# An attention kernel whose V comes in 4 KB rows for three packs in four

## The chip, the cores and the metric

One core of a Trainium2 chip. The time is the device time of one execution in microseconds, lower is better. Where several were timed, the median is given.

## The reference

Two independent attention blocks, A and B, with the same shapes; their outputs are put side by side. For each block:

```python
B, Sq, D, H, Sk, Dh = 16, 64, 640, 32, 512, 128          # all bf16
q = (x @ wq).reshape(B, Sq, H, Dh).transpose(0, 2, 1, 3)
scores = einsum("bhqd,bhkd->bhqk", q, k_cache) * Dh**-0.5
p = softmax(scores, axis=-1)
o = einsum("bhqk,bhkd->bhqd", p, v_cache)
return o.transpose(0, 2, 1, 3).reshape(B, Sq, H * Dh) @ wo
```

The K and V caches are 268 MB together and each byte is used once; this is a kernel that reads.

## The kernel before

Work is cut into 128 packs: two batch rows and four heads each. 32 packs make a phase (16 heads of one block); four phases. Within a phase the pack index `j = n % 4` says which four heads. Each engine has a fixed program; a planner written in Python orders every operation by a guessed time (`AT`, in units of one pack) and derives the waits. The order of the loads on the SP queue is fixed too: the planner simulates the loader with guessed load times and takes, of the loads whose buffer it thinks free, the most urgent.

```python
    AT = dict(..., KT=(-1.051, -0.379), S=0, ..., PV=1.655, ...)
    DMA_US = dict(LDK=1.27, LDV=1.35, LDWQ=1.75, LDWO=1.75, LDX=0.45)
...
            ready = n - cfg.NK + AT["S"] + 0.25 if n >= cfg.NK else -99.0     # NK = 6 packs of K
            loads.append((tk - 0.05, ready, 2, op))
...
            ready = n - cfg.NV + AT["PV"] + 0.2 if n >= cfg.NV else -99.0     # NV = 4 packs of V
            loads.append((tv - 0.05, ready, 3, op))
```

V is laid out so that one row of a transfer is 2 KB, and P times V uses two 64-row tiles of the array:

```python
        def em_LDV(e, op):
            ...
            src = blocks[blk][2][2 * bp + b, h:h + 4].rearrange("(a s) (p t) d -> (s p) a (t d)", s=2, t=8)
            ins = e.dma_start(v_ring[:, n % NV, b].rearrange("p a t d -> p a (t d)"), src)
...
            ...
        def em_PV(e, op):
            ...
            for a in range(2):
                for b in range(2):
                    for t in range(8):
                        for s in range(2):
                            rows = slice(64 * s, 64 * s + 64)
                            col = a * 128 + 64 * b
                            last = e.matmul(o_ps[:, s, col:col + 64], v_ring[rows, n % NV, b, a, t, :],
                                            pT_ring[rows, (2 * n + a) % NT, b, t, :],
                                            start=(t == 0), stop=(t == 7), tile_position=(64 * s, 0))
                            ...
```

K comes as `"h (p t) d -> (h p) (t d)", t=16`: 4 KB rows. PE's program is a prologue, a loop of four packs run 31 times, and an epilogue:

```python
            for op in prog[:lo]:
                emit(e, op, p, {})
            with e.Fori(0, reps):
                ...
            ...
```

Of the kernel before, what the change touches and what calls it, by code (L numbers as in the profile page):

```python
# [17 lines left out]
class Cfg:  # L18
# [5 lines left out]
    NWS = 4  # L24
    NQ = 2
    NP = 2
    NPN = 2
    NT = 2
    NO = 1
    NR = 4  # L30
    PERIOD = 4
    FIRST = 5
    SLOT_US = 5.6
    AT = dict(XT=-2.594, XE=-2.103, XC=-0.826, QP=-0.625, QE=-0.284, KT=(-1.051, -0.379), S=0,
              EX=(0.262, 0.298, 0.389, 0.649), RC=(0.547, 0.697), NM=(0.571, 0.642, 0.8, 1.158), TR=(1.059, 1.236),
              TE=(1.121, 1.538), PV=1.655, OE=1.933, OP=2.167, OA=2.291, OV=2.255, ST=3.374, WP0=-1.75, WP1=-1.488)
    DMA_US = dict(LDK=1.27, LDV=1.35, LDWQ=1.75, LDWO=1.75, LDX=0.45)
# [22 lines left out]
def build_plan(dims, cfg, general):  # L60
# [17 lines left out]
    if not general:  # L78
        add("pool", "INIT1", 0, -10.0, [], [("out_sb", 0)])
        add("pool", "INIT2", 0, -9.9, [("out_sb", 0)], [("ident",)])  # L80
    for g in range(N // NJ + 1):
        n0 = g * NJ
        txt = n0 + AT["XT"]
        add("pe", "XT", g, txt, [("xn", g % cfg.NXN), ("ident",)], [("OUTB",)])
        if g == N // NJ:
            break
        if dims["FIRST"](g // NBP):
            add("act", "XE", g, n0 + AT["XE"], [], [("OUTB",), ("xs", g % NBP)])
            op = add("sp", "LDX", g, txt - 0.5, [], [("xn", g % cfg.NXN)])
            loads.append((txt - 2.4, (g - cfg.NXN) * NJ + AT["XT"] if g > cfg.NXN else -7.0, 0, op))  # L90
        add("pool", "XC", g, n0 + AT["XC"], [("xs", g % NBP)], [("xT", g % cfg.NX)])
    for ph in range(NPH):
        for j in range(NJ):
            w = ph * NJ + j
            n0 = ph * PH + j
            twp = n0 + (AT["WP1"] if ph else AT["WP0"])
            add("pool", "WP", w, twp, [("ws", w % cfg.NWS)], [("wqp", j)])
            op = add("sp", "LDWQ", w, twp - 0.5, [], [("ws", w % cfg.NWS)])
            ready = -99.0
            if w >= cfg.NWS:  # L100
                pw = w - cfg.NWS
                ready = (pw // NJ) * PH + pw % NJ + (AT["WP1"] if pw // NJ else AT["WP0"]) + 0.5
            loads.append((twp - 0.3 if not ph else ready + 2.0 + 0.15 * PH, ready, 1, op))
            tuse = n0 + AT["OE"]
            op = add("sp", "LDWO", w, n0 + AT["OP"] - 0.8 * NJ, [], [("wo", j)])
            ready = n0 - NJ + AT["OP"] + 0.2 if ph else -99.0
            loads.append((tuse - 0.3, ready, 4, op))
    for n in range(N):
# [3 lines left out]
        add("pe", "QP", n, n + AT["QP"], [("xT", g % cfg.NX), ("wqp", j)], [("SB", 0)])  # L112
        add("act", "QE", n, n + AT["QE"], [], [("SB", 0), ("qs", n % cfg.NQ)])
        for b in range(2):
# [3 lines left out]
            ready = n - cfg.NK + AT["S"] + 0.25 if n >= cfg.NK else -99.0  # L118
# [7 lines left out]
        for i in range(4):  # L126
            h = 4 * n + i
            te = n + AT["EX"][i]
            if general:
                add("dve", "MX", h, te - 0.002, [], [("SB", i), ("negmax", h % cfg.NR)])  # L130
            add("act", "EX", h, te, [("negmax", h % cfg.NR)] if general else [],
                [("SB", i), ("p", (h // 2) % cfg.NP, h % 2), ("rs", h)])
            add("pool", "NM", h, n + AT["NM"][i], [("p", (h // 2) % cfg.NP, h % 2), ("recip", (h // 2) % cfg.NR)],
                [("pn", (h // 2) % cfg.NPN, h % 2)])
        for a in range(2):
            m = 2 * n + a
            add("dve", "RC", m, n + AT["RC"][a], [("rs", 2 * m), ("rs", 2 * m + 1)], [("recip", m % cfg.NR)])
            add("pe", "TR", m, n + AT["TR"][a], [("pn", m % cfg.NPN, 0), ("pn", m % cfg.NPN, 1), ("ident",)],
                [("B5",)])
            add("dve", "TE", m, n + AT["TE"][a], [], [("B5",), ("pT", m % cfg.NT)])  # L140
        add("pe", "PV", n, n + AT["PV"], [("pT", (2 * n) % cfg.NT), ("pT", (2 * n + 1) % cfg.NT),
                                          ("v", n % cfg.NV, 0), ("v", n % cfg.NV, 1)], [("B5",), ("OUT1",)])
        add("act", "OE", n, n + AT["OE"], [], [("B5",), ("OUT1",), ("oT", n % cfg.NO)])
        add("pe", "OP", n, n + AT["OP"], [("oT", n % cfg.NO), ("wo", j)], [("OUTB",), ("OUT1",)])
        last = j == NJ - 1
        bp = g % NBP
        add("dve", "OA", n, n + AT["OA"], [("acc", bp, 1)],
            [("OUT1",), ("out_sb", 0) if last and final else ("acc", bp, 1)])
        if last:
            add("dve", "OV", g, n + AT["OV"], [("acc", bp, 0)],  # L150
                [("OUTB",), ("out_sb", 1) if final else ("acc", bp, 0)])
            if final:
                add("act", "ST", g, n + AT["ST"], [("out_sb", 0), ("out_sb", 1)], [("out_dram", g)])
    if not general:
        add("dve", "FL1", 0, N - 1 + AT["RC"][1] + 0.002, [("rs", h) for h in range(4 * N)], [("good",)])
        add("pe", "FLM", 0, N - 1 + AT["TR"][1] + 0.002, [("good",)], [("SB", 0)])
# [37 lines left out]
    lo = next(i for i, o in enumerate(pe) if o.kind == "TR" and o.idx == cfg.FIRST)  # L194
    hi = next(i for i, o in enumerate(pe) if o.kind == "TR" and o.idx == cfg.FIRST + 2 * cfg.PERIOD)
# [3 lines left out]
    step = dict(XT=cfg.PERIOD // NJ, QP=cfg.PERIOD, S=cfg.PERIOD, TR=2 * cfg.PERIOD, PV=cfg.PERIOD, OP=cfg.PERIOD)  # L199
# [7 lines left out]
    for op in ops:  # L207
        if op.kind == "OP":
            at[("OE", op.idx)].deps += [d for d in op.deps if d.kind == "LDWO"]
            op.deps = [d for d in op.deps if d.kind != "LDWO"]  # L210
        if op.kind == "XT" and op.idx > 0:
            hosts = [d for d in op.deps if d.kind == "OV"]
            for d in op.deps:
                if d.kind == "LDX" and hosts:
                    hosts[0].deps.append(d)
            if hosts:
                op.deps = [d for d in op.deps if d.kind != "LDX"]
# [3 lines left out]

    own = {"XC", "QE", "KT", "NM", "TE", "OE", "OA", "OV", "LDV"}

    def for_pe(d):
        if d.kind == "EX":
            return d.idx % 2 == 0
        if d.kind == "OV" and d.idx == N // NJ - 1 or d.kind == "OA" and d.idx == N - 1:
# [3 lines left out]
    def stand_in(d, op):  # L231
        if op.eng == "pe":
            if d.kind == "XE":
                return at[("OE", d.idx * NJ - NJ)] if d.idx else d
# [7 lines left out]
        if d.kind == "NM":  # L242
            return at[("TR", d.idx // 2)]
        if d.kind == "KT":
            return at[("S", d.idx[0])]
        if d.kind == "EX":
            return at[("EX", d.idx + 1)]
        if d.kind in ("OA", "OV"):
            n = d.idx if d.kind == "OA" else d.idx * NJ + NJ - 1
            return at[("OP", n + 1)]  # L250
        if d.kind == "OE":
            return at[("OP", d.idx)]
        if d.kind == "TE":
            return at[("PV", d.idx // 2)]
# [170 lines left out]
def mha_kernel(nc, blocks, out, cfg=None):  # L425
# [4 lines left out]
    assert SQ == 64 and DH == 128 and SK == 512 and D % 128 == 0 and B % 2 == 0 and H % 4 == 0  # L430
    KT = D // 128
    scale = float(DH) ** -0.5
    N0 = min(D, 512)
    N1 = D - N0
    assert 0 < N1 <= 128
# [5 lines left out]
    NH = NBLK * NBP * H  # L441

    plans = []
    for general in (False, True):
        dims = dict(NPH=NPH, NBP=NBP, NJ=NJ, FIRST=lambda ph: ph % NSUB == 0,
                    FINAL=lambda ph: ph % NSUB == NSUB - 1)
        plans.append(build_plan(dims, cfg, general))
    NK, NV, NKT, NX, NXN, NWS, NQ, NP, NPN, NT, NO, NR = (cfg.NK, cfg.NV, cfg.NKT, cfg.NX, cfg.NXN, cfg.NWS, cfg.NQ,
                                                          cfg.NP, cfg.NPN, cfg.NT, cfg.NO, cfg.NR)

    with contextlib.ExitStack() as es:
# [7 lines left out]
        ws_ring = sb("ws_ring", [128, NWS, KT, 512], BF16)  # L459
        kn_ring = sb("kn_ring", [128, NK, 2, 2048], BF16)  # L460
        kt_ring = sb("kt_ring", [128, NKT, 2, 16, 2, 32, 2], BF16)
        v_ring = sb("v_ring", [128, NV, 2, 2, 8, DH], BF16)
# [4 lines left out]
        p_ring = sb("p_ring", [128, NP, 8, 2, 64], BF16)  # L467
        pn_ring = sb("pn_ring", [128, NPN, 8, 2, 64], BF16)
        pT_ring = sb("pT_ring", [128, NT, 2, 8, 64], BF16)
        oT_ring = sb("oT_ring", [128, NO, 2, 2, 128], BF16)  # L470
# [3 lines left out]
        negmax = sb("negmax", [128, NR], F32)  # L474
        recip = sb("recip", [128, NR, 2], F32)
# [12 lines left out]
        PT_BANK, O_BANK, OUT_BANK = 4, 5, 7  # L488
        pt_flat = ps[:, PT_BANK:PT_BANK + 2, :].bitcast(BF16)[:, :, 0:512]
        o_ps = ps[:, O_BANK:O_BANK + 2, :].rearrange("p e c -> p (e c)")[:, 256:768].rearrange("p (s c) -> p s c", s=2)  # L490
        x_ps = ps[:, OUT_BANK, :].bitcast(BF16)
        out_ps0 = ps[:, OUT_BANK, 0:N0]
        out_ps1 = ps[:, O_BANK + 1, 256:256 + N1]
# [14 lines left out]

        def em_LDX(e, op):
# [5 lines left out]
        def em_LDWQ(e, op):  # L515
            c = op.idx % (NSUB * NJ)
            src = blocks[op.idx // (NSUB * NJ)][3].rearrange("(kt p) n -> p kt n", p=128)[:, :, c * 512:(c + 1) * 512]
            ins = e.dma_start(ws_ring[:, op.idx % NWS], src)  # L518
# [15 lines left out]
        def em_LDV(e, op):  # L534
            n, b = op.idx
            blk, bp, j, h = pack_info(n)
            src = blocks[blk][2][2 * bp + b, h:h + 4].rearrange("(a s) (p t) d -> (s p) a (t d)", s=2, t=8)
# [318 lines left out]
```

## Time and profile before

| | before |
|---|---|
| time | 770.06 us (3 runs, 769.87 to 770.34) |
| span of the profiled run | 768.0 us |
| DMA from 100 to 700 us | 395 GB/s, every 19.2 us slice but the last 90% busy or more, or nearly (the first is 8) |
| PE busy | 88% |
| last load lands, and the rest to the end | 756.7 us, 11.3 us |

PE is the engine of the matmuls and PEld its weight loads; DVE, ACT and POOL are VectorE, ScalarE and GpSimd. A ring is a set of buffers used in turn. The tail is the time from the landing of the last load to the end.

In the profile, a line of digits has one digit for each fortieth of the span, in tenths of busy time. "SPq" is the queue that issues loads; its time in the chain of waits means that transfers ahead of it had to be moved first. Landings and packets are single records of the trace. The prediction shows the lines themselves.

### The profile page before, as it was taken

How to read it: one execution, taken by the hardware profiler on the slowest of the kernel's cores; microseconds unless marked ns; L12 is line 12 of the kernel's file. 1: busy time of each engine (PE TensorE's matmuls, PEld its weight loads, DVE VectorE, ACT ScalarE, POOL GpSimd, SP SyncE). 2: the span in 40 equal slices, each digit the busy share in tenths (PEclk: the TensorE clock that was granted, in tenths of full speed). 3: DMA queues.
4: the chain of work that ended last, by engine and by line, in shares of the span. 5: the costliest groups of instructions: out<-in, count | busy, mean ns of one | idle time of the engine just before them, and what ended most of it. 6: DMA issues, size and time to landing. Idle time of an engine off the chain costs nothing.

```text
span 768.0 us, 44433 instructions
## 1 busy us (share of the span) xinstructions
PE 675.2 (88%) x20006; PEld 491.6 (64%) x20134; DVE 545.6 (71%) x934; ACT 483.8 (63%) x1297; POOL 405.9 (53%) x582
## 2 busy tenths in 40 slices
PE   3868999999987799999996779999998799999995
PEld 2546666676765567676765557676766567677764
DVE  3537777777765678787775567777877578788874
ACT  2536676776665567666764557677766566666763
POOL 5525545454954355554694344555568354545452
PEclk9989999999999999999999999999999999999999
DMA  8999999999999999999999999999999999999991
GB/s 312 388 385 386 398 397 398 396 397 398 397 385 388 388 398 400 399 399 399 397 393 391 383 391 397 396 387 398 398 398 391 391 399 398 400 399 399 400 396 60
DMA packets 130094, 295.16 MB, mean 384 GB/s; under 512 B 9216, under 2 KB 31744, under 8 KB 130048
## 3 DMA queue, kind: packets, MB, share of 16 engines
q1 hardware_dynamic: 127744, 292.06, 100.6%
q10 hardware_dynamic: 2304, 2.62, 1.0%
q8 instruction: 12, 0.20, 0.1%
q14 instruction: 34, 0.28, 0.1%
HBM read 292.03 MB, written 2.62 MB: 384 GB/s over the span
## 4 chain that ended last, share of the span: by engine, by line
SPq 55%; DMA 21%; PE 18%; issue 3%; DVE 1%; POOL 0%; ACT 0%; DVEq 0%
SPq L538 26%; SPq L531 25%; DMA v_ring<-in_A_v_cache_dram 11%; DMA v_ring<-in_B_v_cache_dram 6%; PE ps L659 5%; PE ps L573 4%; PE ps L596 3%; PE ps L675 2%; PE ps L640 2%; SPq L512 2%; DMA wo_sb<-in_B_wo_dram 2%; DMA kn_ring<-in_B_k_cache_dram 2%; DMA wo_sb<-in_A_wo_dram 1%; PE ps L678 1%; SPq L518 1%
## 5 line engine op out<-in xcount | busy, mean ns | idle before, releaser
L631 POOL TENSOR_SCALAR pn_ring<-p_ring,recip 128x512 bf16<-128x512 bf16 x512 | 345.7, 695 | 343.3 <-DVE recip L626 343.3
L611 ACT ACTIVATE p_ring<-ps 128x512 bf16<-128x512 f32 x512 | 301.0, 593 | 165.5 <-PE ps L640 162.5
L586 DVE STREAM_TRANSPOSE kt_ring<-kn_ring 128x1024 f32<-128x1024 f32 x256 | 314.5, 1232 | 102.6 <-DMA kn_ring<-in_B_k_cache_dram 56.3
L647 DVE COPY pT_ring<-ps 128x1024 bf16<-128x1024 bf16 x256 | 176.0, 687 | 54.4 <-PE ps L640 47.6
L573 PE MATMUL ps<-xT_ring,wqp_sb 128*128 128x128 bf16 x2560 | 171.0, 223 | 7.9 <-POOL xT_ring L562 5.5
L659 PE MATMUL ps<-pT_ring,v_ring 64*128 64x64 bf16 x8192 | 143.1, 191 | 23.9 <-DMA v_ring<-in_A_v_cache_dram 10.4
L573 PEld LDWEIGHTS ps<-xT_ring,wqp_sb 128*128 128x128 bf16 x2560 | 150.5, 115 | 15.6 <-POOL xT_ring L562 5.7
L659 PEld LDWEIGHTS ps<-pT_ring,v_ring 64*128 64x128 bf16 x8192 | 127.8, 95 | 41.6 <-DMA v_ring<-in_A_v_cache_dram 16.0
L596 PE MATMUL ps<-kt_ring,qs_ring 32*64 32x512 bf16 x4096 | 147.6, 399 | 4.6 <-issue 2.4
L640 PEld LDWEIGHTS ps<-ident,pn_ring 64*128 64x128 bf16 x4096 | 74.6, 95 | 118.7 <-ACT oT_ring L666 60.2
L666 ACT ACTIVATE oT_ring<-ps 128x512 bf16<-128x512 f32 x128 | 76.5, 598 | 99.0 <-PE ps L659 80.6
L678 PE MATMUL ps<-wo_sb,oT_ring 128*128 128x128 bf16 x512 | 112.5, 220 | 21.3 <-issue 18.8
L640 PE MATMUL ps<-ident,pn_ring 64*128 64x64 bf16 x4096 | 105.1, 192 | 26.9 <-DVE pT_ring L647 20.0
L675 PE MATMUL ps<-wo_sb,oT_ring 128*128 128x512 bf16 x384 | 118.8, 381 | 0.0
L611 ACT ACTIVATION_READ_ACCUMULATOR p_ring<-ps 128x1 f32 x512 | 101.7, 199 | 0.0
L675 PEld LDWEIGHTS ps<-wo_sb,oT_ring 128*128 128x128 bf16 x512 | 50.0, 98 | 53.1 <-issue 0.8
L579 ACT ACTIVATE qs_ring<-ps 128x512 bf16<-128x512 f32 x128 | 76.4, 597 | 10.8 <-PE ps L573 10.8
L596 PEld LDWEIGHTS ps<-kt_ring,qs_ring 32*64 32x64 bf16 x4096 | 55.5, 104 | 38.8 <-issue 4.0
L688 DVE TENSOR_TENSOR acc<-acc,ps 128x128 f32<-128x128 f32 x96 | 27.4, 285 | 32.9 <-PE ps L678 32.8
L678 PEld LDWEIGHTS ps<-wo_sb,oT_ring 128*128 128x128 bf16 x512 | 50.4, 98 | 0.0
L626 DVE RECIPROCAL recip<-rowsum 128x2 f32<-128x2 f32 x256 | 35.6, 139 | 2.6 <-ACT p_ring L611 2.6
L545 POOL COPY wqp_sb<-ws_ring 128x1280 bf16<-128x1280 bf16 x16 | 20.0, 1252 | 8.1 <-DMA ws_ring<-in_A_wq_dram 8.1
(24 smaller groups left out, 116.4 us busy)
## 6 DMA issues: line engine op xcount, KB each, us to landing
kn_ring<-in_A_k_cache_dram SPq DMA_DIRECT2D x128, 512.0 KB, 12.5
v_ring<-in_A_v_cache_dram SPq DMA_DIRECT2D x128, 512.0 KB, 12.6
kn_ring<-in_B_k_cache_dram SPq DMA_DIRECT2D x128, 512.0 KB, 12.6
v_ring<-in_B_v_cache_dram SPq DMA_DIRECT2D x128, 512.0 KB, 10.7
ws_ring<-in_A_wq_dram SPq DMA_DIRECT2D x8, 640.0 KB, 11.7
wo_sb<-in_A_wo_dram SPq DMA_DIRECT2D x8, 640.0 KB, 12.2
ws_ring<-in_B_wq_dram SPq DMA_DIRECT2D x8, 640.0 KB, 12.2
wo_sb<-in_B_wo_dram SPq DMA_DIRECT2D x8, 640.0 KB, 12.6
```

The costliest lines, as they stand in the source:

```text
L531: ins = e.dma_start(kn_ring[:, n % NK, b, :], src)
L538: ins = e.dma_start(v_ring[:, n % NV, b].rearrange("p a t d -> p a (t d)"), src)
L573: last = e.matmul(ps[:, 0, f * 128:(f + 1) * 128], w[:, kt, f, :], xT_ring[:, xs, kt, :], start=(kt == 0), stop=(kt == KT - 1))
L586: ins = e.transpose(dst, kn_ring[:, n % NK, b, :].bitcast(F32))
L596: last = e.matmul(ps[64 * b:64 * b + 64, i, :], qs_ring[rows, n % NQ, f, b, :], kt_ring[rows, n % NKT, b, :, f // 2, :, f % 2], start=(f = ...
L611: ins = e.activation(dst, src, ACTF.Exp, scale=1.0, accum_out=rowsum[:, h:h + 1])
L631: ins = e.tensor_scalar(pn_ring[:, (h // 2) % NPN, :, h % 2, :], p_ring[:, (h // 2) % NP, :, h % 2, :], recip[:, (h // 2) % NR, h % 2:h % ...
L640: last = e.transpose(pt_flat[:, b, 64 * t:64 * t + 64], pn_ring[rows, op.idx % NPN, t].rearrange("q s k -> q (s k)"), ident[rows, rows], t ...
L647: ins = e.tensor_copy(pT_ring[:, op.idx % NT].rearrange("p b t q -> p b (t q)"), pt_flat)
L659: last = e.matmul(o_ps[:, s, col:col + 64], v_ring[rows, n % NV, b, a, t, :], pT_ring[rows, (2 * n + a) % NT, b, t, :], start=(t == 0), st ...
L675: last = e.matmul(out_ps0, oT, wo_sb[:, 4 * j + h4, 0:N0], start=(j == 0 and h4 == 0), stop=(j == NJ - 1 and h4 == 3))
L678: last = e.matmul(out_ps1, oT, wo_sb[:, 4 * j + h4, N0:D], start=(h4 == 0), stop=(h4 == 3))
```

## The change

The intent: V's rows of 2 KB cost more DMA time per byte than K's of 4 KB, and DMA binds. For `j` in 0, 1, 2 V is now laid out as K is. The 4 KB rows put a head on 32 partitions, so P times V is done by four 32-row tiles. The change puts the results of the four row tiles in four PSUM banks. Two of these are shared with the output projection, which keeps accumulating in them; in these two the part for P times V is zeroed by ScalarE and accumulated into without a start flag. wq comes in 4 KB rows in three of the four phases.

```diff
+    PAD = 80
+    WIDE = (0, 1, 2)
-    AT = dict(..., KT=(-1.051, -0.379), S=0, ..., PV=1.655, OE=1.933, OP=2.167, ...)
-    DMA_US = dict(LDK=1.27, LDV=1.35, LDWQ=1.75, LDWO=1.75, LDX=0.45)
+    AT = dict(..., KT=(-1.24, -1.0), S=0, ..., PV=1.75, OE=(2.0, 2.06), ZO=2.11, OP=2.31, ...)
+    DMA_US = dict(LDK=1.27, LDV=1.29, LDWQ=1.5, LDWO=1.75, LDX=0.45)
...
-            ready = n - cfg.NK + AT["S"] + 0.25 if n >= cfg.NK else -99.0
+            ready = n - cfg.NK + AT["KT"][b] + 0.25 if n >= cfg.NK else -99.0
...
         def em_LDV(e, op):
...
+            if j in WIDE:
+                ins = e.dma_start(dst.rearrange("p t d -> p (t d)"), src.rearrange("h (p t) d -> (h p) (t d)", t=16))
+            else:
+                ins = e.dma_start(dst.rearrange("p (a t) d -> p a (t d)", a=2), ...)          # as before
...
         def em_PV(e, op):
...
+            tall, tiles, per = (32, 4, 16) if wide else (64, 2, 8)
+            for a in range(4 // tiles):
+                for b in range(2):
+                    for t in range(per):
+                        for s in range(tiles):
+                            rows = slice(tall * s, tall * s + tall)
+                            i, c = a * tiles + s, a * per + t
+                            last = e.matmul(ps[:, 4 + i, 64 * b:64 * b + 64], v_ring[rows, n % NV, b, c, :],
+                                            pT_sb[rows, b, c, :], start=(t == 0 and i < 2), stop=(t == per - 1),
+                                            tile_position=(tall * s, 0), skip_group_check=i >= 2)
...
+        def em_ZO(e, op):
+            ins = e.activation(z_ps, zeros[:, :].rearrange("p (s c) -> p s c", s=2), ACTF.Copy)
...
         def em_LDWQ(e, op):
...
+            if ph:
+                ins = e.dma_start(ws_sb[:, i].rearrange("p j c -> p (j c)"), src[:, i, c:c + NJ * 512])
...
         def run_program(e, eng, p):                        # PE only
+            for _ in range(0 if p else cfg.PAD):
+                e.sem_inc(s_fl, 1)
```

Beside these, all transposes of a pack are one run of 32, the exps of wide packs write plain rows, and the output is added up once in four packs.

## The prediction

> **What bounds the kernel now.** I first read the busy line of the DMA engines over the span, then the packets.
>
> ```profile
> PE   3868999999987799999996779999998799999995
> ...
> DMA  8999999999999999999999999999999999999991
> GB/s 312 388 385 386 398 397 398 396 397 398 397 385 388 388 398 400 399 399 399 397 393 391 383 391 397 396 387 398 398 398 391 391 399 398 400 399 399 400 396 60
> DMA packets 130094, 295.16 MB, mean 384 GB/s; under 512 B 9216, under 2 KB 31744, under 8 KB 130048
> ```
>
> The DMA line is 9 from the second slice (19.2 us each) to the last but one; PE dips to 6 and 7 near slices 12, 22 and 31, where a new set of weights is loaded. The chain of waits agrees:
>
> ```profile
> SPq 55%; DMA 21%; PE 18%; issue 3%; DVE 1%; POOL 0%; ACT 0%; DVEq 0%
> ```
>
> 76% of it is the load queue and its transfers. The list of waits says that the queue itself hardly waits for buffers (PV 1.9 us, scores 0.8 us, 20.5 us for the small x buffer, with transfers still queued behind it). So the rings always have room, and the time is the sum of what the 16 DMA engines move, plus a start and an end. Bytes don't change; only cost per byte can.
>
> That cost I took from the packet records of the trace. Mean durations: 1024 B 50.6 ns, 1280 B 58.9, 2048 B 87.9, 4096 B 164.7. Packets of one engine overlap by about 4 ns (an engine starts 2048 B packets every 80 ns though each shows 84). A least-squares fit of packet counts in 1 to 4 us windows against elapsed time gives 46.9, 55.4, 84.3 and 161 ns. With these the DMA work is 747.5 us of the 768.0, leaving 20.5 for start and end. The landing times are a second measure: K (512 KB in 4 KB rows) lands a median 1.282 us after the load before it (mean 1.299), a pair of V (2 KB rows) 2.706 (mean 2.752), so 1.353 each; wq (640 KB in 1 KB rows) 1.857.
>
> PE is second, and close. From the timeline of one undisturbed pack:
>
> ```profile
> 154.26 1.11 PE L659 MATMUL ps<-pT_ring,v_ring 64*128 64x64 bf16 x64
> ...
> 155.30 1.14 PE L596 MATMUL ps<-kt_ring,qs_ring 32*64 32x512 bf16 x32
> ...
> 156.37 0.41 PE L640 MATMUL ps<-ident,pn_ring 64*128 64x64 bf16 x16
> ...
> 157.90 0.41 PE L640 MATMUL ps<-ident,pn_ring 64*128 64x64 bf16 x16
> ...
> 158.24 1.31 PE L573 MATMUL ps<-xT_ring,wqp_sb 128*128 128x128 bf16 x20
> ...
> 159.54 1.11 PE L659 MATMUL ps<-pT_ring,v_ring 64*128 64x64 bf16 x64
> ```
>
> PV to PV is 5.28 us with PE nearly solid. Starts of PV run 5.25, 5.4, 5.27, 5.5 (mean 5.36) away from weight loads and 7.1 beside them. K and V of one pack cost DMA 2 x 1.282 + 2.706 = 5.27. Inside a phase of 32 packs PE and DMA are therefore about level; weights, x and output put DMA ahead as the bound.
>
> **What the Trainium skill says.**
> 1. "Perfetto Trace Analysis", DMA Optimizations: going from 2 KB to 4 KB or more "can dramatically improve throughput". The trace agrees in direction; its own gain is only 2 x 84.3 against 161, under 5%.
> 2. "DMA: Bandwidth & Descriptors", Why small descriptors are slow: some 3 cycles of overhead per packet on top of one per 32 B. By that estimate 2 x 67 cycles become 131, 2.2%; the trace shows about twice that, and I use the trace.
> 3. "TensorE: Matmul & The Clock Gate", Part 3, The mechanism: matmuls on different row tiles start about 4 ns apart and overlap. The trace agrees: two PV tiles start 3 ns apart and each pair takes 29.2 ns; eight score tiles start 3.3 ns apart.
> 4. "Runtime: NRT & Kernel Launch", Instruction fetch mechanics: PE holds 2048 instructions in blocks of 256, and a branch outside what is held stalls. In this trace the instruction queue moved 0.28 MB, while PE ran 40,140 loads and matmuls (2.6 MB at 64 B), so PE's loop is held. For the new loop, see the rivals.
>
> **The change, part by part.**
> *V.* 3 packs in 4 are 192 of 256 loads. Each goes from 1.353 to what K takes, 1.282, since its access pattern becomes K's: 192 x 0.071 = 13.6 us by medians. By means 192 x 0.077 = 14.8. By the packet fit, 24,576 packets of 4 KB save 2 x 84.3 - 161 = 7.6 ns each: 24,576 x 7.6 / 16 = 11.7 us. I take 13.6.
> *wq.* In three of four phases, 4 loads of 1.857 (7.43) become 5 of 512 KB in 4 KB rows (5 x 1.282 = 6.41): 3 x 1.02 = 3.0 us.
> *PV on PE.* A wide pack has 128 matmuls in place of 64, but four row tiles instead of two run together. If four starts (4 x 3.3 = 13 ns) fit in the 29.2 ns of one 64-column pass, it is still 32 x 29.2 = 0.93 us plus the drain, as now. The extra cost is zero if loads and matmuls are issued at 3.65 ns each over 256 instructions; the trace proves 7.3 ns sustained, less only in short bursts.
> *Rest of PE.* Transposes of a pack become one run of 32: 16 x 29.2 + 0.12 = 0.59 us, in place of 0.41 twice with a wait of 0.16 between the first and the output projection. Output projection stays at 2560 columns (1.07 us). Order S, TR, OP, QP, PV: 1.07 + 0.59 + 1.09 + 1.31 + 1.04 = 5.10 against 5.28. With the x transposes that come once in four packs I expect some 5.2 against 5.36.
> *ACT.* One eviction of 0.60 becomes two of 128x256 and the zeroing. From 0.698 at 640 columns and 0.597 at 512, an estimate of 0.39 each, 1.18 in all: +0.6 us a pack on 483.8 / 128 = 3.78. Both banks must be read and zeroed before OP: done about 1.25 us after PV ends, while scores and transposes keep PE busy 1.66 us. It fits.
> *DVE.* The 0.29 us add of every pack becomes one of about 0.82 (an estimate from 0.285 at 128 and 0.69 at 512 columns) every fourth: less work. *POOL* keeps four multiplies of 0.695 a pack; the first now waits for three exps, not two. From the start of scores: 1.25 to the first exp, 2.1 for three, 0.2 for the reciprocal, 2.8 for POOL = 6.35, against transposes due at 5.10 + 1.07 = 6.17. Nearly level, up to 0.2 us of wait.
> *Start and end.* 80 semaphore increments on PE (51 ns each, as PE's others) are 4 us in which DMA has its first loads anyway; no V buffer is waited for before 45 us. The end after the last scores is 16.6 us now; the new chain (1.14 scores, 2.4 exps, 3.0, 0.9 transposes, 1.5 copies, 1.2 PV, 1.2 ACT, 1.35 OP, 0.9 DVE, 2.7 store, 1.2 close) is 17.5: +0.9.
>
> Sum: 770.06 - 13.6 - 3.0 + 0.9 = 754.4; the pace of PE in the last phase, which sets how far it lags at the end, may give back one: 26 packs x 0.16 us would be 4 us, of which I book 0.8. **753.6 us**, 2.1% faster.
>
> **Rivals.**
> *PE becomes the bound.* If 128 small matmuls cost twice 64, a wide pack takes 5.2 + 1.04, the mean is 5.2 + 0.75 x 1.04 = 5.98, and 128 x 5.98 + 36 of filling and emptying is about 801: slower by 4%. For it: PE is at 88%, and only 3 packs in 4 were made wide. Against it: starts 3.3 ns apart over eight tiles in the scores. At 7.3 ns an instruction PV would be near 1.5 us and PE's mean 5.55: DMA mostly hides it, but PE lags at the end by up to 26 x 0.38 = 10 us: 760 to 764.
> *Loop no longer held.* I count 4 x (20 + 32 + 32 + 8) + 3 x 128 + 64 + 5 = 821 matmuls, 1642 instructions with weight loads, and some 26 more: under 2048, about 6.5 blocks. Four wide packs would reach 7 blocks, which explains the choice of three and the padding. If it did refetch, 107 KB and a stall of 1 us or more in each of some 30 turns: 765 or more.
> *V's slowness is not its rows.* If the 7 ns per 4 KB came from interference between reads and not from row size, half would remain: 762.
> *PE's shorter pack helps too.* Then rings stay fuller, but DMA still binds: no more than 2 us, 751.
>
> **Range and chances.** The two measures of row cost span 11.7 to 14.8 us for V; with wq, 14.7 to 17.8; end and lag add -3 to +6. That gives 748 to 762. The 2% line, 754.7, is 1.1 us above the centre, so it is nearly a coin toss: faster 0.57, within 2% 0.41, slower 0.02 for the first two rivals.
>
> **What would show it.** Right: the packet counts fall by 24,576 (V) and 5,760 (wq), 4096 B packets keep near 164 ns, GB/s inside a phase rises from 398 to 404 or so, DMA stays at 9, PV of wide packs takes 1.1 us for 128 matmuls, PE's pack is 5.1 to 5.3. Wrong: PV of 1.5 us or more; the DMA line falling to 7 or 8 inside a phase (PE binds); instruction-queue traffic in every loop turn; waits of OP for the zeroing; 4 KB packets of 170 ns; a tail longer than 19 us.

## The result, and the profile after

The changed kernel takes 772.99 us (4 runs, 772.21 to 773.97), beside 770.2 for the kernel before on the same chip: a ratio of 1.0037, 95% interval 1.0019 to 1.0054. The prediction said 753.6, in a range of 748 to 762.

The page of the changed kernel, the same lines as shown of before:

```profile
PE   1667699999999999999989989999999899899995
...
DMA  5999899999999999999999999999999999999960
GB/s 200 388 396 406 300 408 405 406 406 407 407 398 398 407 407 407 407 409 407 406 403 393 406 408 406 405 406 405 406 407 396 389 407 408 407 408 407 407 263 15
DMA packets 99810, 295.22 MB, mean 383 GB/s; under 512 B 9264, under 2 KB 24112, under 8 KB 99760
...
SPq 34%; PE 29%; DMA 19%; POOL 7%; issue 6%; DVE 4%; ACT 1%; POOLq 0%; ACTq 0%; DVEq 0%
```

The middle is what was predicted: 404 to 408 GB/s in most slices in place of 396 to 400. Three places are new: the first slice moves 200 GB/s instead of 312, the fifth 300, and the last but one 263 where there were 396. Transfers are faster, and the mean over the span is still 383 against 384.

The gain of single transfers came, to the figure. A pair of wide V loads lands a median 2.57 us after what went before (2.706 for the narrow ones of the kernel before), wq's 15 loads 1.280 each (1.857 for the 12 before). 4096-byte packets took 163.9 ns on average, 59,264 of them instead of 32,768. (In a kernel that mixes both, landings alone don't tell the rows apart well: its narrow pairs land after 2.67 us, and after 2.56 in the run with all three mends below. What wide rows are worth rests on the runs with and without them.)

The three losses, each with the view that shows it. First, the start. From the timeline of PE (start, duration, what ran; in brackets the idle time before it and what it waited for):

```profile
13.21 0.69 PE L567 MATMUL ps<-ident,xn_ring 128*128 128x128 bf16 x5 [13.21 <-issue]
```

PE's first matmul comes at 13.2 us instead of 3.2. Ahead of it stand the 80 increments, one every 151 ns: the trace shows each as busy for 51 ns and says nothing of the rest. The load of the second x block waits for this matmul, because there is one x buffer, and every load behind it in the queue waits as well. From the list of waits of the load queue (total us, times, longest):

```profile
SPq L516 <- PE ps L567: 10.0, 1, 10.0
```

Second, the first pass through PE's program. More of PE's timeline, changed kernel:

```profile
35.75 1.43 PE L611 MATMUL ps<-kt_ring,qs_ring 32*64 32x512 bf16 x17 [4.04 <-issue]
...
48.16 0.38 PE L669 MATMUL ps<-ident,pn_sb 64*128 64x64 bf16 x14 [3.81 <-issue]
...
54.75 0.51 PE L690 MATMUL ps<-pT_sb,v_ring 32*128 32x64 bf16 x44 [1.60 <-issue]
...
60.99 0.66 PE L588 MATMUL ps<-xT_ring,wqp_sb 128*128 128x128 bf16 x9 [2.27 <-issue]
...
67.10 0.45 PE L669 MATMUL ps<-ident,pn_sb 64*128 64x64 bf16 x10 [2.92 <-issue]
```

PE stops in the middle of runs of matmuls, waiting for nothing that has a semaphore. Counted over all its instructions, the stops lie at the 705th, 961st, 1217th, 1473rd, 1729th, 1985th, 2497th and 2753rd: multiples of 256 apart. The DMA queue that the page lists as the eighth moves one packet of 16,384 bytes, 256 instructions, per stop. The page of before, then of the changed kernel:

```profile
q8 instruction: 12, 0.20, 0.1%
```

```profile
q8 instruction: 15, 0.25, 0.1%
```

The packets of the first pass start some 6.3 us apart (33.3, 39.6, 45.8, 52.2, 58.4, 64.7 us and on to 87.1), and the kernel before has the same stops, one per 255 or 256 instructions, with packets as far apart, the last at 70.0. So PE runs the first pass at 256 instructions per 6.3 us while loads fill the DMA queues. A narrow pack has 312 instructions, a wide one 440. The scores of pack 8 start at 71.8 us before and at 93.1 us after. The rings fill, and the load queue waits (37 waits of up to 10.9 us for the scores in the whole run, against two of up to 0.6 us before):

```profile
SPq L539 <- PE ps L611: 113.1, 37, 10.9
```

Third, the end. The table of stretches (us, then busy time of PE, weight loads, DVE, ACT and POOL with counts, granted clock, DMA share, GB/s), before and then after, cut where the last load lands:

```profile
700.00:756.00 56.00, 53.34 (x1633) 39.14 (x1642) 43.34 (x78) 38.81 (x108) 28.98 (x43) 1.00 0.95 362
756.00:768.00 12.00, 4.51 (x142) 3.14 (x135) 4.50 (x11) 1.19 (x2) 2.05 (x4) 0.96 0.09 24
```

```profile
700.00:736.00 36.00, 34.76 (x1400) 27.44 (x1393) 26.56 (x43) 26.62 (x82) 18.50 (x28) 1.00 1.03 407
736.00:750.60 14.60, 14.20 (x544) 10.83 (x531) 11.35 (x18) 11.18 (x35) 7.04 (x11) 1.00 0.62 233
750.60:770.50 19.90, 11.94 (x460) 8.54 (x457) 5.63 (x16) 6.14 (x20) 5.38 (x8) 0.89 0.05 14
```

Loads end 6.1 us earlier, and 19.9 us of work follow where 11.3 did; in the 14.6 us before, DMA is at 0.62. The landings say why. In packs 116 to 124 of the changed kernel K lands 14.3 to 15.1 us before its scores start, but V only 0.0 to 3.1 us before P times V; before, 3.8 to 4.1 and 0.0 to 0.3. The order in which the trace has the loads issued: when V of pack n is issued in the last phase, K of n+2 has been issued before the change; after it the lead grows in the phase from 2 packs to 4, which it has from pack 112 on. K far ahead is of no use to PE, which needs both. When K is done, only V of the last packs is left; it lands fast (2.5 us a pack), and PE then works off those packs at 5.3 us each.

The middle of the run pays for the start: between packs 8 and 96 the changed kernel gains 20.5 us (93.1 to 578.6 against 71.8 to 577.8), so at pack 96 it is 0.8 us behind.

### The profile page after: what moved, and what is told of

Read it like the earlier page. It is cut to its first block, busy times and chain, and to the rows that moved or that the text cites. A ratio compares the mean times of both kernels' runs of the same rounds, so it can differ in the third digit from the quotient of the medians.

```text
span 770.5 us, 56929 instructions
## 1 busy us (share of the span) xinstructions
PE 685.8 (89%) x26278; PEld 528.9 (69%) x26278; DVE 520.5 (68%) x806; ACT 517.8 (67%) x1554; POOL 405.0 (53%) x583
## 4 chain that ended last, share of the span: by engine, by line
SPq 34%; PE 29%; DMA 19%; POOL 7%; issue 6%; DVE 4%; ACT 1%; POOLq 0%; ACTq 0%; DVEq 0%
SPq L539 15%; DMA v_ring<-in_B_v_cache_dram 11%; SPq L548 10%; PE ps L690 7%; PE ps L710 6%; SPq L550 6%; POOL pn_sb L658 6%; PE ps L588 6%; PE ps L611 6%; PE ps L669 4%; DMA kn_ring<-in_A_k_cache_dram 2%; DVE pT_sb L676 2%; DMA v_ring<-in_A_v_cache_dram 2%; SPq L516 2%; DMA kn_ring<-in_B_k_cache_dram 1%
## 5 line engine op out<-in xcount | busy, mean ns | idle before, releaser
L658 POOL TENSOR_SCALAR pn_sb<-p_ring,recip 128x512 bf16<-128x512 bf16 x512 | 344.5, 692 | 337.9 <-DVE recip L645 337.9
L676 DVE COPY pT_sb<-ps 128x1024 bf16<-128x1024 bf16 x256 | 164.2, 683 | 137.8 <-PE ps L669 137.5
L690 PE MATMUL ps<-pT_sb,v_ring 32*128 32x64 bf16 x14336 | 154.7, 193 | 27.5 <-DMA v_ring<-in_B_v_cache_dram 10.2
L690 PEld LDWEIGHTS ps<-pT_sb,v_ring 32*128 32x128 bf16 x14336 | 140.2, 92 | 42.5 <-DMA v_ring<-in_B_v_cache_dram 16.8
L710 PE MATMUL ps<-wo_sb,oT_sb 128*128 128x320 bf16 x1024 | 165.1, 305 | 1.0 <-ACT ps L702 1.0
L698 ACT ACTIVATE oT_sb<-ps 128x256 bf16<-128x256 f32 x256 | 84.3, 381 | 115.3 <-PE ps L690 102.9
L669 PEld LDWEIGHTS ps<-ident,pn_sb 64*128 64x128 bf16 x4096 | 70.7, 96 | 85.8 <-ACT ps L702 51.2
L710 PEld LDWEIGHTS ps<-wo_sb,oT_sb 128*128 128x128 bf16 x1024 | 90.9, 99 | 38.7 <-ACT ps L702 1.2
L669 PE MATMUL ps<-ident,pn_sb 64*128 64x64 bf16 x4096 | 84.4, 192 | 25.1 <-POOL pn_sb L658 12.7
L702 ACT ACTIVATE ps<-zeros 128x256 f32<-128x256 bf16 x129 | 50.9, 395 | 0.0
L567 PE MATMUL ps<-ident,xn_ring 128*128 128x128 bf16 x165 | 15.4, 227 | 13.2 <-issue 13.2
## 6 DMA issues: line engine op xcount, KB each, us to landing
kn_ring<-in_A_k_cache_dram SPq DMA_DIRECT2D x128, 512.0 KB, 12.2
ws_sb<-in_B_wq_dram SPq DMA_DIRECT2D x10, 512.0 KB, 13.6
```

The lines of the kernel that those rows point to most:

```text
L658: ins = e.tensor_scalar(dst, src, recip[:, h // 4 % NR, i:i + 1], 1.0, ALU.mult, ALU.mult)
L669: last = e.transpose(pt_bank(b)[:, 64 * c:64 * c + 64], pn_sb[rows, c, :], ident[rows, rows], tile_position=(64 * b, 0))
L676: ins = e.tensor_copy(pT_sb[:, b].rearrange("p t q -> p (t q)"), pt_bank(b))
L690: last = e.matmul(ps[:, 4 + i, 64 * b:64 * b + 64], v_ring[rows, n % NV, b, c, :], pT_sb[rows, b, c, :], start=(t == 0 and i < 2), stop=(t ...
L698: ins = e.activation(oT_sb[:, 2 * a:2 * a + 2, :], o_ps[:, 2 * a:2 * a + 2, :], ACTF.Copy)
L710: last = e.matmul(out_ps[:, s, :], oT_sb[:, i, :], wo_sb[:, 4 * j + i, s * NH0:(s + 1) * NH0], start=(j == 0 and i == 0), stop=(j == NJ - ...
```

## The experiments

All were timed in three rounds beside the kernel before, which took 769.8 to 770.1 us in each set. All outputs are right. Theory: the transfers gained what was predicted, and three separate things gave it back: the padding at PE's start, the first pass through a longer program, and the order of the loads. Rivals: the padding is idle decoration; or PE's own pace with small tiles is the cause throughout.

**The padding away.**

```diff
-    PAD = 80
+    PAD = 0
```

> The 80 semaphore increments ahead of PE's program are taken away, nothing else. Theory A (they only delay PE by 12.2 us, so the second x load waits and DMA idles some 5.7 us between 8 and 20 us; the loop stays held in PE's instruction memory, 8 blocks of 256 instead of 7): DMA full from 5 us on, 765 to 769 us. Rival B (the padding keeps the loop inside 7 blocks; with 8 it is fetched anew in each turn): PE shows stalls of 2 to 6 us every 256 instructions through the whole run, 8 a turn, over 31 turns: 950 us or more.

1392.12 us. My theory was wrong for this run and the rival right ("950 us or more"). The loop has 1660 instructions; with the padding it begins 31 instructions into a block and touches 7 blocks, without it 207 into one and touches 8. Eight blocks are not held:

```profile
PE   5665666566665667675675656766567676566756
...
DMA  9966556465655765655675557655566565555541
...
q8 instruction: 285, 4.67, 1.4%
```

285 packets instead of 15, some nine a turn. PE shows the same stops in the later turns too, up to 4.6 us between 600 and 645 us. The padding is needed; its cost is not. This run also bears on the 6.3 us of a block: from 600 to 619 us, where loads move about half of what they move when nothing holds them up, block follows block in 3.1 to 3.8 us. So busy DMA engines seem to be part of what a block costs; no run changed that alone.

**The same 80 increments, later.**

```diff
-            for _ in range(0 if p else cfg.PAD):
-                e.sem_inc(s_fl, 1)
             for op in prog[:lo]:
                 emit(e, op, p, {})
+                if op.kind == "XT" and op.idx == 0:
+                    for _ in range(pad):
+                        e.sem_inc(s_fl, 1)
```

> The same 80 increments, after the first x transposes instead of before them: the second x load no longer waits, PE's first projection is as late as in the changed kernel (15 to 16 us). If the idle DMA of 8 to 20 us costs: DMA loses under 1 us there and the time is 766 to 769. If not DMA but the lateness of PE costs: within 1.5 us of the changed kernel, 771.5 to 774.5.

770.63 us (767.19 to 771.35), between the two expectations and with a wide spread. DMA is no longer idle at first (329 GB/s over the first 24 us against 230, and 326 before), but it loses more between 72 and 100 us (295 GB/s against 335): the rings fill sooner, since PE is nearly as late as it was (pack 8 starts at 90.7 us). Inconclusive as to which of the two counts; it shows that load time won at the start is lost again while PE is late.

**Padding that costs little.** Forty matmuls into a bank not yet used, with their weight loads also 80 instructions:

```diff
+                if op.kind == "XT" and op.idx == 0:
+                    for _ in range(pad // 2):
+                        e.matmul(ps[:, 3, 0:64], ident[:, :], ident[:, 0:64], start=True, stop=True)
```

> 40 idle matmuls with their weight loads (80 instructions, about 4 us cold) after the first x transposes, in place of the 80 increments: same place of the loop, PE's first projection back at about 9.5 us and DMA not held up. Theory: 764 to 768, a little under the run with the late increments, because PE also reaches its instruction stalls 6 us earlier. Rival (start does not matter, the end is set elsewhere): 771 to 774.

765.82 us (765.65 to 768.20), 7.2 under the changed kernel; as expected. The forty start 53 ns apart, some 2.1 us in all. Scores of pack 8 start at 88.5 us. (The profiled execution is the slowest of the four, 768.20.)

**The order of the loads alone.**

```diff
-    DMA_US = dict(LDK=1.27, LDV=1.29, LDWQ=1.5, LDWO=1.75, LDX=0.45)
+    DMA_US = dict(LDK=1.35, LDV=1.40, LDWQ=1.75, LDWO=1.75, LDX=0.45)
```

> Only the planner's guesses of load times change (K 1.35, V 1.40, wq 1.75 us), so the fixed order of the loads: K runs 2 packs ahead of V instead of 3 to 4. Theory (K taken too early pushes V late, PE waits for V inside the phases, and the last V loads and their packs are left over): from the last load's landing to the end 11 to 14 us instead of 20.4, 763 to 768 us. Rival (the end is PE's own pace over the last ten packs, whatever the order): 772 to 774, tail shorter only because the loads end later.

770.25 us, 2.7 less: neither number. The tail falls from 19.9 to 15.0 us, not to 11 to 14, and K's lead over the scores to 5 us in the last phase, but DMA moves 336 GB/s between 84 and 128 us instead of 362, a loss of nearly 3 us more. The order is part of the end; the rest of the longer tail is not explained by it.

**Both.**

> Idle matmuls for padding and the planner's slower load times together. If the start and the order of the loads are separate costs, the two gains add (7.2 and 2.7 us): 762 to 764.5. If the order mattered only because PE was late at the start: no more than the idle matmuls alone, 765 to 767.

765.32 us (763.12 to 766.62): here the gains do not add, as far as this spread tells; DMA still moves only 273 GB/s in its fifth slice. Why the order gives only 0.5 us here is open: it gave 2.7 where PE was later still.

**One fetched block less.** The padding of idle matmuls, and the first two packs narrow. Their code lies before the loop, so this takes 2 x 128 = 256 instructions from the first pass and leaves the loop's place within a block as it was:

```diff
+        def wide_pack(n):
+            return n >= 2 and n % NJ in WIDE
```

(used in place of `j in WIDE` in the V load, exp, normalising and P times V.)

> Idle matmuls for padding, and the first two packs narrow (2 KB rows, two 64-row tiles), so PE has 256 instructions, one fetched block, fewer before its loop. Theory (in the first pass PE advances one block of 256 instructions per 6.3 us, so the count of instructions sets its lateness): the start of the scores of pack 8 comes 5.5 to 6.5 us earlier than in the run with idle matmuls alone (88.5 us), DMA loses 0 to 2 us at 70 to 92 us instead of 5.5, time 760 to 763. Rival (lateness from the cold clock or from waits for data): pack 8 within 2 us of 88.5, time 765 to 767.

762.21 us. Pack 8 starts at 82.7 us, 5.8 earlier for one block less, and DMA moves 401 GB/s between 72 and 100 us where it had moved 321. The table of stretches, with idle matmuls alone and then with one block less:

```profile
72.00:100.00 28.00, 21.58 (x782) 16.17 (x779) 14.89 (x24) 14.62 (x45) 11.14 (x17) 0.82 0.84 321
```

```profile
72.00:100.00 28.00, 24.25 (x880) 17.82 (x882) 15.93 (x25) 17.43 (x53) 11.32 (x17) 0.86 1.03 401
```

A trade of 2 MB in slower rows for 256 fewer instructions wins 3.6 us. The work of a pack on PE can't be the reason: P times V of a wide pack takes 1.21 us and of a narrow one 1.11. The fetch is shown.

**All three.**

> All three mends together. If they add: 756 to 761, the best so far, and 1.2 to 1.8% under the kernel before. If PE's own pace in the last phase (5.3 us a pack) is what is left: 761 to 763.

759.04 us (757.59 to 759.69), ratio 0.9852 (0.9835 to 0.9868). The order is now worth 3.2 us. The tail is 15.3 us.

**The change without wide packs.**

```diff
-    WIDE = (0, 1, 2)
+    WIDE = ()
-    PAD = 80
+    PAD = 0
```

> The change without its wide packs (V in 2 KB rows, two tiles everywhere) and without padding, which its loop of 1276 instructions does not need; order of the loads as in the change. DMA work returns by the V term (12 to 15 us), the first pass is back at the length of the kernel before. Theory (DMA binds, V rows are worth 12 to 15 us, the start of the changed kernel costs as much): 766 to 771. Rival (rows of V are worth little, the new structure itself costs): 773 or more, or, if the rows cost nothing and only the start did: under 762.

773.52 us. A miss: slower than expected, and than the kernel before; taken alone it falls in the range of the rival, that V's rows are worth little. DMA is full from the first to the last slice but two, and loads end at 753.6 us, 3.1 earlier than before, which is wq's gain; but 18.0 us follow, with K 14 us ahead in the last packs. This pointed to the order again, free of wide packs and of a late start. Two runs settle it.

**The kernel before with the planner's figures of the change.** No operation changes, only the order of its loads; load times were set low, to give K a lead of 4 packs:

```diff
-            ready = n - cfg.NK + AT["S"] + 0.25 if n >= cfg.NK else -99.0
+            ready = n - cfg.NK + AT["KT"][b] + 0.25 if n >= cfg.NK else -99.0
-    DMA_US = dict(LDK=1.27, LDV=1.35, LDWQ=1.75, ...)
+    DMA_US = dict(LDK=1.20, LDV=1.22, LDWQ=1.5, ...)
```

> The kernel before with nothing but the planner's figures of the change (K buffer thought free after its transpose, faster loads: K 1.20, V 1.22, wq 1.5 us), so that K runs 4 packs ahead of V in the last phase instead of 2. Theory (K ahead of V is lead that PE can't use: V comes just in time and its packs are left over at the end): tail from the last load's landing 16 to 20 us instead of 11.3, time 774 to 778. Rival (the order costs only together with wide packs or a late PE): within 1.5 us of 770.

774.19 us, ratio 1.0050 (1.0033 to 1.0067). Loads end 0.9 us earlier, the tail is 16.7 us instead of 11.3. By the trace K leads by 3.5 packs in most of every phase, so this is not quite the changed kernel's order, and PE is 4.6 us late already at pack 96. But it shows that such an order alone costs, here 4.4 us, in a kernel that has nothing else of the change.

**Narrow packs with the slower planner times.**

> The changed kernel with narrow packs only, no padding, and the planner's slower load times. Theory: the order cost 4 to 7 us of the narrow run's 773.5, so 766 to 770; the difference to the wide run with all mends (759.0) is then V's rows alone, 8 to 11 us. Rival (the narrow run is slow for another reason, its new PE order): 772 to 774.

770.22 us, just above the expected 766 to 770. The order cost 3.3 us here. The distance to the run with all three mends, 770.22 - 759.04 = 11.2 us, is what the wide packs bring, net of what they cost PE; the expectation said 8 to 11. Loads end 11.3 us apart (742.6 against 753.9), with the same tail but for 0.8 us. It also shows that the rest of the change is worth nothing by itself: wq's 3 us come (loads end at 753.9), and the tail is 14.5 us.

**The best run.** All three mends, and K's buffer counted free after the scores, as in the kernel before (that is when the load really may start: its wait is on the scores).

> The best run so far (idle matmuls, two narrow packs at the start, slower planner times) with the K buffer counted free after the scores as in the kernel before, so K leads by 2 to 3 packs in the first phase too. If the order in the first phase matters: 756 to 758.5. If PE, late by 9 to 13 us through the first phase, hides it: 758.5 to 760.

758.81 us (758.70 to 759.28), ratio 0.9852 (0.9836 to 0.9868): level with the run with all three mends. It says little about the order in the first phase: by the trace only 25 of 563 loads have changed places, and K leads by 2 packs in most of it in both runs. It beats the kernel before by 11 us and the changed one by 14, 1.5 and 1.8%. Its page:

```profile
PE   4775999999999999999997889999999799999995
...
DMA  8999999999999999999999999999999999999980
```

## Why the prediction was wrong

*What bounds, and the transfers: right.* Each V load in 4 KB rows was to save 0.071 us: 1.353 became 1.28. wq was to save 3.0 us: 12 x 1.857 - 15 x 1.280 = 3.1. Net, V is worth 11.2 us against 13.6 in the sum; the four loads kept narrow are 0.3 of the difference, and how the rest divides no run says.

*PE with four tiles: right.* 128 matmuls of a wide pack take 1.21 us, predicted 1.1; PE's pack is 5.29 on average (medians from one P times V to the next, away from weight loads: 5.37, 5.50, 5.10, 5.20), predicted 5.2. The rival of a doubled cost did not come. The Trainium skill's starts of about 4 ns apart for different row tiles ("TensorE: Matmul & The Clock Gate", Part 3, The mechanism) hold for 128 matmuls in a row: in pack 40 most starts within a group of four are 2 to 5 ns apart, and a group takes (1.21 - 0.19) / 32 = 32 ns.

*The failing step: start and end.* The sum said "80 semaphore increments on PE (51 ns each, as PE's others) are 4 us in which DMA has its first loads anyway". They took 12.2 us, because 51 ns is what the record shows and 151 ns the distance; and the loads were not independent of PE, since the second x load waits for its first transposes. Cheap padding of the same length gained 7.2 us. Of the prediction's own signs of being wrong, the tail over 19 us came (19.9), and DMA fell to 8 in the fifth slice, but not because PE binds. That the time stayed within 2%, to which it gave 0.41, is luck: it meant a gain just short of 2%. (The terms of its range give 749 to 761, not 748 to 762; neither reaches 773.)

*A cost that was missing.* The prediction counted the loop's instructions to see whether it is held, and got that right; even its reason for three wide packs in four and for the padding fits the run without padding, though the limit lies higher: 7 blocks touched are held, 8 are not. It didn't ask how PE gets through the code the first time. It read another instruction queue, too: the 0.28 MB are those of q14, while the packets that go with PE's stops are those of q8 (0.20 MB), which leads to the same answer. With 256 instructions per 6.3 us, the first pass of some 2900 instructions instead of 2170 costs PE 3 blocks, about 18 us, of which DMA lost some 5 while the rings were full (335 GB/s for 28 us, where 405 was the rule); one block taken away gained 3.6 us. The change's own diff held the count.

*The end, sized too small.* The sum had +0.9 for the chain after the last scores (16.6 to 17.5; measured 17.8) and gave 0.8 back for PE's pace. What was missing is the planner: two figures of guessed load times and one of a buffer's free time, in the diff but read as bookkeeping, moved K from 2 packs ahead of V to 4 at the end. Before, the last scores start 5.3 us before the last load lands, and now 2.1 us after it; that, and not the chain behind the scores, is most of the longer tail. An order of this kind alone costs the kernel before 4.4 us; mended in the changed one beside the other two it returns 3.2.

Added up in medians: 772.99 - 7.2 - 3.6 - 3.2 - 0.2 = 758.8 (each run adds one mend to the one before it, so the steps must add up; in another order they may be of other sizes). The remaining 5.2 us to the predicted 753.6 are about the 2.4 of V's term and a tail of 15.1 us where 11.3 + 0.9 - 0.8 was assumed, 3.7; that is 0.9 too much, half of it because the profiled execution took 759.28. Why this tail stays longer with the order mended is seen in part in the traces. V still lands 6.9 us before the last P times V, against 3.3 before. Of these 3.6, 1.4 are there at pack 125 already (1.7 against 0.3), 1.2 come because the V of the last two packs lands in 5.4 us instead of 6.6, and 1.1 because PE needs 10.7 us for these two packs instead of 9.6. The last pack takes 6.4 us (4.7 before) with narrow packs too, so that share isn't the small tiles'. No run took this apart.

## What to carry to other kernels

When a transfer gets cheaper in a kernel with deep rings, the gain is only had if the consumer is on time at both ends of the run: look at the first pass through the code, where instructions themselves are loaded by DMA beside the data, and at which tensors are in hand when the last load lands. Read changes to a static planner's guesses as changes to the program: compare the order that comes out of it. And take an instruction's cost from the distance to the next one, not from the length of its record.

## What the Trainium skill lacked or had wrong

- "Runtime: NRT & Kernel Launch", Instruction fetch mechanics, calls the crossing of a 16 KiB block "mostly hidden". Here, with loads queued, PE got one block of 256 instructions per 6.3 us in its first pass and stood still for 1.6 to 4.0 us at most crossings.
- The same section speaks both of 2048 instructions for PE and of only two lines held. Here a loop touching 7 blocks was held for 31 turns (15 fetched blocks in the run), and one touching 8 was not (285 blocks, 1392 us).
- No page was found that gives the cost of an increment that PE's sequencer issues by itself: 151 ns from one to the next, 51 ns in the record. It would belong to "Perfetto Trace Analysis", Sequencer-only Instruction, which says only that such a record leaves out the wait for a semaphore and the way of its update.
- "DMA: Bandwidth & Descriptors", Why small descriptors are slow, gives some 3 cycles a packet, an estimate of 2.2% from 2 KB to 4 KB rows; the landings give 1.353 against 1.28 us per 512 KB, 5%. "Perfetto Trace Analysis", DMA Optimizations, says that such a step "can dramatically improve throughput".
